# Beta factors loaded behind B's value weights, and phi's max(b,0) moved from VectorE to ScalarE

## The chip, the cores and the metric

The kernel runs on one core of one Trainium2 chip. The metric is the device time of one execution in microseconds (us); a kernel's time is the median of its runs. The core has five engines that run side by side, each through its own list of instructions in order: TensorE (PE; its weight loads are shown as PEld), VectorE (DVE), ScalarE (ACT), GpSimd (POOL) and SyncE (SP). DMA transfers are issued by SP, POOL or ACT and run on 16 DMA engines.

## The reference: what is computed

Two attention blocks over the same 2048 rows of 512 values, 32 heads of 16, mixed by a gate per row:

```python
x = A_x
g = _sigmoid((x * gate_w).sum(-1, keepdims=True))
a = _A_ref(x, A_wq, A_wk, A_wv, A_wo, A_beta)
b = _B_ref(x, B_wqkv, B_wo)
return g * a + (1 - g) * b
```

B is plain softmax attention over all 2048 rows. A works in four chunks of 512 rows. Inside a chunk it is causal attention (each row looks at itself and the rows ahead of it); across chunks a memory is carried, read with phi(q) and updated with phi(k):

```python
phi = lambda t: jnp.where(t > 0, t + 1.0, jnp.exp(t))
...
    num = jnp.einsum("bhld,bhde->bhle", pq, M)
    den = jnp.einsum("bhld,bhd->bhl", pq, z)[..., None] + 1e-6
    a_mem = num / den
    o = g * a_mem + (1.0 - g) * a_dot
    pk = phi(ks)
    M = M + jnp.einsum("bhld,bhle->bhde", pk, vs)
```

Here g is the sigmoid of one number per head, `A_beta`. In the kernel phi(t) is written as max(t,0) + min(exp(t),1), which is the same function.

## The kernel before: tiles, stages, queues

The order of the instructions on every engine is the order in which the code emits them; waits are put in where an instruction reads or overwrites what another engine made. There are three stages.

**Opening (to about 78 us).** x is loaded, A's values are projected, x is split in a high and a low half-precision part scaled by its largest absolute value. Then eight jobs `qk_job(3, "B", 0, w, c)` (L877) project B's queries and keys of the first group of heads. Beside them stand the preparations for what follows. Behind the third of these jobs VectorE takes the largest absolute values of A's first weights (`w_abs("A", 0)`, L884) and of the four pieces of B's value weights, k = 0 to 3 (`peak`, L366); behind the fourth, `top(("A", 0))` (L890) sends the result through a TensorE transpose (L383). TensorE's list goes no further before that one has run.

The four pieces of B's value weights are loaded by POOL (`load_wv`, L277), pieces 0 and 1 in the loop ahead (at `tt == 12`), pieces 2 and 3 behind the first qk_job (L881). Pieces 2 and 3 go into buffers that hold x's second chunk until VectorE has split its first half (L265). POOL's DMAs are issued in order, and an issue also waits until the eighth POOL DMA ahead of it has landed, since they share eight semaphores. On the same queue stand:

- `load_beta` (L225), twelve small DMAs that spread `A_beta` over the partitions into `gh` (4, L227) and `nq` (8, L230); `do_beta` (L235) makes the gate factors of them in the first block of the middle stage;
- `axk`, four DMAs `kb<-aux` (L181) that write constant rows into key buffer KB[0], which the score matmuls of the middle stage read;
- two more `qb<-aux` DMAs and, behind everything, the loads of A's second group of weights (L285).

**Middle stage (about 78 to 347 us).** Sixteen blocks, `blk` = 4 groups of heads x 4 chunks (L925). Each block projects A's queries (w = 0) and keys (w = 1) of its group and chunk with twelve matmuls each (L332), and between them runs the memory steps (`mem_out` reads the memory with phi(q): matmuls L436; `mem_tr` transposes phi(k): L461; `mem_upd`: L475, L480, L483), B's value projections (`v_job`, L302), B's other queries and keys, and from block 4 on first score maxima (`s_b`: matmuls L574, VectorE maximum L576). The function `qk_out` (L336) empties the PSUM bank b of a projection. Of the queries' and keys' 32 projections for A, 24 need phi. For such a one, before:

1. VectorE (L345): `ph = max(b*un, 0)`, from the bank;
2. ScalarE (L346): the high part `st[:, 0] = b*sc`, from the bank;
3. ScalarE (L348): `ex = exp(b*un)`, from the bank;
4. VectorE (L349): the low part `st[:, 1] = b*sc - st[:, 0]`, from the bank, after which the bank is free;
5. VectorE (L351): phi's sum `ph = min(ex, 1) + ph`, from SBUF, which `mem_out` or `mem_tr` reads.

Two engines never read one bank at a time: waits between the steps keep them in turn. `phe` (ex) has one buffer, phi one for w = 0 and one for w = 1, and `st` four, which come free when their two stores by SP (L355) have landed. From block 4 on the projections have four banks (tb, tb, mb, pvb), taken in the order in which they were last used.

**Main stage (from about 347 us).** 32 rounds, each with one unit of A's and one of B's attention: score matmuls L637, exponentials on ScalarE L643, value matmuls L659, and the next units' score maxima on VectorE (L576, L560, L562). Nothing of the change stands there.

Of the kernel before, what the change touches and what calls it, by code (L numbers as in the profile page):

```python
# [12 lines left out]
AF = mybir.ActivationFunctionType  # L13
OP = mybir.AluOpType
# [25 lines left out]
def gated_mix_kernel(ctx, tc, xt, wq, wk, wv, wo, beta, wqkv, wob, gate_w, out):  # L40
    nc = tc.nc
# [93 lines left out]
    def raw_buf():  # L135
        i = cnt.get("raw", 0)
        cnt["raw"] = i + 1
        return RAWV[i if i < 6 else 6 + (i - 6) % 8]
# [62 lines left out]
    def first_x(c, ks):  # L201
        first_split(xh[0][:, c % 2, ks], xl[c % 2][:, ks], XS[c][:, ks])
# [22 lines left out]
    def load_beta():  # L225
        for g in range(4):
            nc.gpsimd.dma_start(gh[:, g:g + 1], bass.AP(tensor=beta.tensor, offset=beta.offset + 8 * g,  # L227
                                                       ap=[[1, 8], [0, E], [1, 1]]))
        for qd in range(8):
            nc.gpsimd.dma_start(nq[:, qd:qd + 1], bass.AP(tensor=beta.tensor, offset=beta.offset + 4 * qd,  # L230
                                                         ap=[[1, 4], [0, 32], [1, 1]]))
# [35 lines left out]
    def wcols(kd, w):  # L267
        if kd == "A":
            return (wq, wk, wv)[w], 0
        return wqkv, w * DM  # L270
# [3 lines left out]
    def load_wv(kd, k, eng=None):  # L274
        src, c0 = wcols(kd, 2)
        WR[kd, "v", k] = raw_buf()
        (eng or nc.gpsimd).dma_start(WR[kd, "v", k], src[k * 128:(k + 1) * 128, c0:c0 + DM])  # L277
# [20 lines left out]
    def v_mm(b, kd, tt, n):  # L298
        xi, wi = TERMS[n // 4]
        c, tl = divmod(tt, 4)  # L300
        x = (XH, XL)[xi][c] if kd == "B" else (xh[0][:, c % 2], xl[c % 2])[xi]
        nc.tensor.matmul(b, x[:, n % 4, tl * 128:(tl + 1) * 128], (WVA if kd == "A" else WV)[wi][:, n % 4, :],  # L302
                         start=n == 0, stop=n == 11)

    def v_out(b, kd, tt):
        tl = tt % 4
        if tl % 2 == 0:
            rot("vs", VS)
        vs = VS[(cnt["vs"] - 1) % 2]
        b = b.rearrange("p (h e) -> p h e", h=H)  # L310
        if kd == "A":
            nc.scalar.activation(vs[:, tl % 2, :, :E], b, AF.Copy)
        else:
            nc.scalar.activation(vs[:, tl % 2, :, :E], b, AF.Copy, scale=vr[:, tt // 4:tt // 4 + 1])
        if tl % 2:
            nc.sync.dma_start(VD[kd][tt * 128 - 128:(tt + 1) * 128].rearrange("(a t) g h e -> t a (g h e)", a=2),
                              vs.rearrange("p a h e -> p a (h e)"))

    def v_job(kd, tt):
        b = misc()  # L320
        for n in range(12):
            v_mm(b, kd, tt, n)
        v_out(b, kd, tt)
# [12 lines left out]
    def qk_out(b, kd, g, w, c):  # L336

        sc = xr[:, c:c + 1]
        st = X.tile([128, 2, C], HF, name="st", bufs=4)
        phi = kd == "A" and (c > 0 if w == 0 else c < NC4 - 1)  # L340
        if phi:
            ph = PHI[g, w, c] = X.tile([128, C], FT, name=f"phi{w}")
            ex = X.tile([128, C], FT, name="phe")
            un = back[:, g, w, c:c + 1]
            nc.vector.tensor_scalar(ph, b, un, 0.0, op0=OP.mult, op1=OP.max)  # L345
        nc.scalar.activation(st[:, 0], b, AF.Copy, scale=sc)  # L346
        if phi:
            nc.scalar.activation(ex, b, AF.Exp, scale=un)  # L348
        nc.vector.scalar_tensor_tensor(st[:, 1], b, sc, st[:, 0], op0=OP.mult, op1=OP.subtract)  # L349
        if phi:  # L350
            nc.vector.scalar_tensor_tensor(ph, ex, 1.0, ph, op0=OP.min, op1=OP.add)  # L351
        img = QKD[kd, w, g][:, :, c * C:(c + 1) * C]
        for a in range(2):
            r = E * (a if w else 1 - a)
            nc.sync.dma_start(img[:, r:r + E], st[:, a])  # L355
        if w == 0 and c == 0:
            nc.sync.dma_start(QKD[kd, w, g][:, 2 * E:].rearrange("h r (n t) -> h r n t", t=64),
                              aux[:, 1, None, :].to_broadcast([E, 2 * NT, 64]))
# [14 lines left out]
    def x_abs(c):  # L373
        peak(stat(("B", 0), 6)[:, 2 + c:3 + c], XS[c])
# [421 lines left out]
    def todo(fn, *a):  # L796
        return lambda: fn(*a)
# [29 lines left out]
    axk = [todo(set_aux, KB[0][:, p], 0) for p in range(2)]  # L827
# [3 lines left out]
    for tt in range(NT):  # L831
        c, tl = divmod(tt, 4)
        if tt < 4:
            for n in range(4, 12):
                v_mm(vb[tt], "A", tt, n)
            v_out(vb[tt], "A", tt)
        else:
            v_job("A", tt)
        if c < 3 and tl < 2:
            first_x(c + 1, halves[tl])  # L840
        if tt in (1, 2, 5, 6):
            x_abs((1, 2, 5, 6).index(tt))
        if tt == 4:
            w_abs("B", 0)
        if tt == 9:
            top(("B", 0))
        if tt == 10:
            w_rng("B", 0)
            split_x(0, halves[0])
        if tt == 11:  # L850
            split_x(0, halves[1])
            x_all()
            w_esc("B", 0)
        if tt == 12:
            split_w(3, "B", 0)
        if tt in (13, 14):
            split_x(1, halves[tt - 13])
        if tt == 3:
            dot_x(0)
        if tt in (7, 12, 15):  # L860
            dot_x({7: 1, 12: 2, 15: 3}[tt])
        if tt == 11:
            load_w("A", 0)
        if tt == 12:
            load_wv("B", 0)
            load_wv("B", 1)
        if tt == 13:
            load_beta()
        if tt == 15:
            split_x(2, halves[0])  # L870
        if ax:
            ax.pop(0)()
    for f in axk:
        f()
    for n in range(8):
        c, w = divmod(n, 2)
        qk_job(3, "B", 0, w, c)  # L877
        if n < 3:
            split_x(2 + (n + 1) // 2, halves[(n + 1) % 2])
        if n == 0:  # L880
            load_wv("B", 2)  # L881
            load_wv("B", 3)
        if n == 2:
            w_abs("A", 0)  # L884
            for k in range(4):
                peak(s8[:, k:k + 1], WR["B", "v", k], AX.X)
            nc.vector.tensor_reduce(stat(("A", 0), 3)[:, 2:3], s8, axis=AX.X, op=OP.max)
            ST["A", 0] = ST["A", 0][0], 3
        if n == 3:
            top(("A", 0))  # L890
        if n == 4:
            w_rng("A", 0)
            split_w(0, "A", 0, (0,))
        if n == 5:
            w_esc("A", 0)
            v_rng()
            split_w(0, "A", 0, (1,))
        if n > 5:
            split_wv(2 * n - 12)
            split_wv(2 * n - 11)  # L900
        if n == 7:
            do_gate()
# [223 lines left out]
    ex = [extras(k) for k in range(32)]  # L1126
# [91 lines left out]
```

## Time and profile before

| | |
|---|---|
| median of 3 runs | 1846.14 us (1845.54 to 1846.72) |
| the profiled execution, its own time | 1847.55 us |
| its span in the trace | 1845.7 us |
| PE busy | 1790.1 us, 97% |
| DVE busy | 1607.8 us, 87% |
| ACT busy | 1445.5 us, 78% |
| POOL busy | 339.6 us, 18% |
| mean granted TensorE clock | 0.994 |

Times in the trace count from the span's start. A row of a timeline has start, length, engine, line, operation, what it writes and reads (out<-in), and in brackets how long its engine sat idle ahead of it and what ended that. A row of the waits has the waiting instruction, the one it waited for, the sum of us, how many times, and the longest. A row of the windows has, for a stretch, its length and the busy us of PE, PEld, DVE, ACT and POOL, then the clock granted to TensorE as a share of full speed. Rows that merge several instructions give their count (x8).

### The profile page before, as it was taken

What the parts mean: (1) busy time and instruction counts of PE and PEld (TensorE: products, weight loads), DVE (VectorE), ACT (ScalarE), POOL (GpSimd) and SP (SyncE); (2) the same over time, 40 slices, a digit from 0 to 9 for tenths busy, and PEclk for the clock granted to TensorE, in tenths of its full rate; (3) what the DMA queues carried; (4) which work ended last, traced back from release to release, by engine and by line L of the source; (5) the groups of instructions that cost most, each with busy time, mean ns of one, the idle gap of its engine ahead of it and who ended that gap; (6) DMA issues with size and microseconds to landing.
All of it is one profiled execution on the core that took longest, in us unless ns stands there. A gap on an engine that the chain in (4) does not pass through costs nothing.

```text
span 1845.7 us, 44303 instructions
## 1 busy us (share of the span) xinstructions
PE 1790.1 (97%) x17781; PEld 644.8 (35%) x17781; DVE 1607.8 (87%) x1811; ACT 1445.5 (78%) x2717; POOL 339.6 (18%) x691
## 2 busy tenths in 40 slices
PE   8799989899999999999999999999999999999998
PEld 6454444322222222333333333333333333333325
DVE  7645786699999999999999999999999999999942
ACT  4433333388989999989898989898989898989894
POOL 4400000101212010212121212121212121212122
PEclk9899999999999999999999999999999999999999
DMA  5645533332323222223232323232323232323111
GB/s 194 130 127 151 159 87 107 91 98 74 93 73 92 63 82 62 80 67 86 67 86 67 85 67 86 68 86 67 86 68 86 68 86 68 87 69 87 46 39 61
DMA packets 162482, 158.92 MB, mean 86 GB/s; under 512 B 40140, under 2 KB 126620, under 8 KB 162276
## 3 DMA queue, kind: packets, MB, share of 16 engines
q1 hardware_dynamic: 158692, 149.29, 29.1%
q0 software_dynamic: 3296, 6.27, 1.8%
q8 instruction: 140, 2.29, 0.5%
q14 instruction: 66, 0.54, 0.1%
q10 hardware_dynamic: 288, 0.52, 0.1%
HBM read 103.38 MB, written 50.86 MB: 84 GB/s over the span
## 4 chain that ended last, share of the span: by engine, by line
PE 72%; DVE 19%; ACT 5%; issue 2%; DMA 2%; SPq 0%; ACTq 0%; DVEq 0%; POOLq 0%
PE pvb L659 27%; DVE mxb L576 14%; PE tb L637 11%; PE sbk L574 9%; PE mb L637 6%; ACT raw L643 3%; PE tb L744 2%; PE tb L332 2%; PE sbk L552 2%; PE mb L332 2%; PE tb L302 1%; PE pvb L332 1%; PE mb L744 1%; PE sbk L302 1%; PE sbk L332 1%
## 5 line engine op out<-in xcount | busy, mean ns | idle before, releaser
L576 DVE TENSOR_REDUCE mxb<-sbk 128x2 f32<-128x1024 f32 x1024 | 1172.3, 1211 | 21.1 <-PE sbk L574 10.4
L643 ACT ACTIVATE raw<-tb 128x512 f32<-128x512 f32 x1555 | 884.1, 600 | 62.6 <-PE tb L637 25.6
L659 PE MATMUL pvb<-raw,vb 128*17 128x256 f32 (+1 forms) x8072 | 644.6, 388 | 0.0
L574 PE MATMUL sbk<-kb,qb 64*128 64x512 f16 x2048 | 552.9, 377 | 9.2 <-DVE mxb L576 8.2
L643 ACT ACTIVATE raw<-mb 128x512 f32<-128x512 f32 x782 | 469.1, 600 | 32.9 <-PE mb L637 16.9
L637 PE MATMUL tb<-qb,kb 64*128 64x512 f16 x1342 | 467.7, 380 | 2.4 <-ACT raw L643 1.3
L637 PEld LDWEIGHTS <-kb 64*128 64x128 f16 x2048 | 143.2, 93 | 413.3 <-issue 409.3
L659 PEld LDWEIGHTS pvb<-raw,vb 128*17 128x17 f32 x8072 | 137.9, 95 | 402.9 <-issue 393.6
L637 PE MATMUL mb<-qb,kb 64*128 64x512 f16 x679 | 258.4, 381 | 0.0
L646 POOL TENSOR_SCALAR_AFFINE_SELECT raw<-raw 128x256 f32<-128x256 f32 (+1 forms) x320 | 115.4, 361 | 324.3 <-ACT raw L643 315.9
L574 PEld LDWEIGHTS <-qb 64*128 64x128 f16 x2048 | 137.1, 93 | 45.6 <-issue 35.2
L560 DVE TENSOR_REDUCE mx<-sbk 128x2 f32<-128x1024 f32 (+1 forms) x128 | 133.9, 1087 | 6.7 <-PE sbk L556 5.6
L659 PE MATMUL pvb<-raw,va 128*17 128x256 f32 (+2 forms) x1280 | 103.2, 383 | 3.7 <-ACT pvs L668 0.9
L703 POOL TENSOR_TENSOR o<-o,d 128x512 f32<-128x512 f32 x31 | 39.4, 1272 | 218.7 <-DMA d<-rd 156.9
L562 DVE TENSOR_REDUCE mx<-sbk 128x4 f32<-128x512 f32 x64 | 60.6, 947 | 12.5 <-PE sbk L556 12.5
L552 PE MATMUL sbk<-ka,qa 64*128 64x512 f16 (+3 forms) x512 | 70.8, 296 | 0.0
L346 ACT ACTIVATE st<-tb,xr 128x512 f16<-128x512 f32 x28 | 19.2, 687 | 59.2 <-DVE phi L345 30.3
L637 PE MATMUL tb<-qa,ka 64*128 64x512 f16 (+3 forms) x339 | 62.0, 302 | 0.0
L691 POOL TENSOR_TENSOR rec<-rec,grow 128x16 f32<-128x16 f32 x24 | 5.3, 222 | 275.7 <-DVE rec L683 275.7
L332 PEld LDWEIGHTS <-ws 128*128 128x128 f16 x384 | 37.6, 99 | 44.5 <-issue 4.8
L556 PE MATMUL sbk<-cmask,crows 64*128 64x64 bf16 x1024 | 52.8, 189 | 0.0
L556 PEld LDWEIGHTS <-crows 64*128 64x128 bf16 x1024 | 46.5, 94 | 13.8
(358 smaller groups left out, 1621.8 us busy)
## 6 DMA issues: line engine op xcount, KB each, us to landing
vb<-vdB SPq DMA_DIRECT2D x16, 1088.0 KB
pd<-pvs SPq DMA_DIRECT2D x64, 256.0 KB
kb<-dB SPq DMA_DIRECT2D x60, 256.0 KB
dB<-st SPq DMA_DIRECT2D x64, 128.0 KB
dA<-st SPq DMA_DIRECT2D x64, 128.0 KB
o<-pd SPq DMA_DIRECT2D x64, 128.0 KB
d<-rd SPq DMA_DIRECT2D x63, 128.0 KB
kb<-dB SPq DMA_DIRECT2D x60, 128.0 KB
```

The source lines that it names most:

```text
L332: nc.tensor.matmul(b, WS[ws][w][wi][:, k, :], (XH, XL)[xi][c][:, k, :], start=n == 0, stop=n == 11)
L552: nc.tensor.matmul(b[:, j, c0:c0 + n], q_of(u)[r, p, i * 128:(i + 1) * 128], k_of(u, p)[r, :n], start=True, stop=False)
L556: nc.tensor.matmul(b[:, j, c0 + n - 128 + w.start:c0 + n - 128 + w.stop], crows[r, n2 - 1], cmask[r, n2 - 1, w], start=False, stop=n2 == 2)
L560: nc.vector.tensor_reduce(m[:, :, p, i], b[:, :, :n], axis=AX.X, op=OP.max)
L562: nc.vector.tensor_reduce(m[:, :, :, i], b.rearrange("q j (p k) -> q j p k", p=2)[:, :, :, :n], axis=AX.X, op=OP.max)
L574: nc.tensor.matmul(b[:, j], q_of(u)[r, p, i * 128:(i + 1) * 128], k_of(u, p)[r, kc * C:(kc + 1) * C], start=True, stop=True)
L576: nc.vector.tensor_reduce(MXB[u][:, :, p, i, kc], b, axis=AX.X, op=OP.max)
L637: nc.tensor.matmul(bs[j][:, c0:c0 + w], k_of(u, h // 2)[r, 128 * it:128 * it + 128], q_of(u)[r, h // 2, q0:], start=True, stop=True)
L643: nc.scalar.activation(pt, bs[j], AF.Exp, scale=AT["esc", kd, qd // 2])
L646: nc.gpsimd.affine_select(out=m, in_=m, pattern=[[1, 128]] if n < 2 else [[0, 2], [1, 128]], compare_op=OP.is_ge, fill=0.0, base=0, channe ...
L659: nc.tensor.matmul(PVB[32 * h:32 * h + E + 1, q0 + lo:q0 + hi], vt[:, it, 4 * q + h, :], pt[:, lo:hi], start=it == 0 and lo == 0, stop=it ...
L744: nc.tensor.matmul(b[j], (AT["oh"], AT["ol"])[oi][r, g, a], (AT["wh"], AT["wl"])[wi][r, g, a], start=n == 0, stop=n == 11)
```

## The change

Two things are moved, and nothing else: what is computed stays the same.

**The loads.** `load_beta` and `axk` are taken from where they stood and put behind `load_wv("B", 2)` and `load_wv("B", 3)`.

**qk_out.** Step 1 goes to ScalarE as a Relu with the same scale, in front of the exponential; the high part comes behind both, and phi's sum ahead of the low part.

```diff
             un = back[:, g, w, c:c + 1]
-            nc.vector.tensor_scalar(ph, b, un, 0.0, op0=OP.mult, op1=OP.max)
+            nc.scalar.activation(ph, b, AF.Relu, scale=un)
+            nc.scalar.activation(ex, b, AF.Exp, scale=un)
+            nc.vector.scalar_tensor_tensor(ph, ex, 1.0, ph, op0=OP.min, op1=OP.add)
         nc.scalar.activation(st[:, 0], b, AF.Copy, scale=sc)
-        if phi:
-            nc.scalar.activation(ex, b, AF.Exp, scale=un)
         nc.vector.scalar_tensor_tensor(st[:, 1], b, sc, st[:, 0], op0=OP.mult, op1=OP.subtract)
-        if phi:
-            nc.vector.scalar_tensor_tensor(ph, ex, 1.0, ph, op0=OP.min, op1=OP.add)
...
-        if tt == 13:
-            load_beta()
...
-    for f in axk:
-        f()
...
         if n == 0:
             load_wv("B", 2)
             load_wv("B", 3)
+            for f in axk:
+                f()
+            load_beta()
```

How POOL's list changes in the opening (a count behind x merges equal issues; `raw<-in_B_wqkv` 128x512 are the value weights' pieces, `in_A_wq` and `in_A_wk` A's weights):

```order
 L277 DMA raw_86<-in_B_wqkv_dram 128x512 x2
-L181 DMA qb_70<-aux 16x8x64 x2
+L181 DMA qb_70<-aux 16x8x64 x4
+L277 DMA raw_86<-in_B_wqkv_dram 128x512 x2
+L181 DMA kb_89<-aux 16x32x64 x4
 L227 DMA gh<-in_A_beta_dram 128x1x1 x4
 L230 DMA nq<-in_A_beta_dram 128x1x1 x8
-L181 DMA qb_70<-aux 16x8x64 x2
-L181 DMA kb_89<-aux 16x32x64 x4
-L277 DMA raw_86<-in_B_wqkv_dram 128x512 x2
 L285 DMA raw_86<-in_A_wq_dram 128x4x128
```

Pieces 2 and 3 stood behind 18 other DMAs after pieces 0 and 1; now four `qb<-aux` stand between, and the twelve beta loads and the four `kb<-aux` come behind.

VectorE's list in block 2, where the bank tb1 holds the queries' and the bank mb the keys' projection, before:

```order
L345 TENSOR_SCALAR phi0_988<-tb1_135,back_128 128x512
L349 SCALAR_TENSOR_TENSOR st_987<-tb1_135,xr_126,st_987 128x512
L351 SCALAR_TENSOR_TENSOR phi0_988<-phe_989,phi0_988 128x512
L345 TENSOR_SCALAR phi1_1018<-mb_137,back_128 128x512
L349 SCALAR_TENSOR_TENSOR st_1017<-mb_137,xr_126,st_1017 128x512
L351 SCALAR_TENSOR_TENSOR phi1_1018<-phe_1019,phi1_1018 128x512
```

and after, in the changed kernel's line numbers (L347 is phi's sum there):

```order
L481 TENSOR_TENSOR mtmp_970<-tb0_134,bmask_115 128x136
L347 SCALAR_TENSOR_TENSOR phi0_988<-phe_989,phi0_988 128x512
L349 SCALAR_TENSOR_TENSOR st_987<-tb1_135,xr_126,st_987 128x512
L347 SCALAR_TENSOR_TENSOR phi1_1018<-phe_1019,phi1_1018 128x512
L349 SCALAR_TENSOR_TENSOR st_1017<-mb_137,xr_126,st_1017 128x512
```

VectorE has one operation less for each of the two, and phi's sum stands ahead of the low part. ScalarE's list at the same place, after (L345 is the Relu, L346 the exponential, L348 the high part, L436 and L437 the copies of `mem_out`):

```order
L345 ACTIVATE phi0_988<-tb1_135,back_128 128x512
L346 ACTIVATE phe_989<-tb1_135,back_128 128x512
L348 ACTIVATE st_987<-tb1_135,xr_126 128x512
L345 ACTIVATE phi1_1018<-mb_137,back_128 128x512
L346 ACTIVATE phe_1019<-mb_137,back_128 128x512
L348 ACTIVATE st_1017<-mb_137,xr_126 128x512
L436 ACTIVATE recm_1028<-sbk0_138 128x16
```

Before it had the high part and the exponential for each, in that order; now three operations follow each other on ScalarE ahead of the copies of `mem_out`.

## The prediction

> **What bounds the kernel now.** I read the windows by stage first, then what TensorE waits for in the opening and middle stages, then the timelines at the longest waits. The windows:
>
> ```profile
> 66.70:78.30 11.60, 0.03 (x1) 0.03 (x2) 4.45 (x9) 0.69 (x1) 3.88 (x6) 0.72 0.75 182
> 78.30:347.00 268.70, 252.35 (x1339) 128.14 (x1340) 171.64 (x320) 96.19 (x189) 15.87 (x26) 0.98 0.43 122
> 347.00:374.00 27.00, 22.98 (x143) 7.38 (x142) 16.52 (x17) 12.64 (x22) 0.00 (x0) 0.94 0.20 57
> 374.00:1800.00 1426.00, 1414.74 (x15822) 442.57 (x15818) 1352.76 (x1364) 1284.04 (x2421) 275.67 (x569) 1.00 0.28 76
> ```
>
> From 66.7 to 78.3 TensorE stands still. From there to 347 it is busy 252.35 of 268.70 us, VectorE only 64%, ScalarE 36%: TensorE's list sets the pace and its idle time is 16.35 us. In the main stage TensorE (99%) and VectorE (95%) are full, and the change touches nothing there; each round starts from what the round ahead left, so an earlier start should move the end by as much. So the question is how much of 11.6 + 16.35 us goes. TensorE's waits from 60 to 347 us (those of at least 1 us in a row):
>
> ```profile
> PE pvb L383 <- DVE stat L887: 11.6, 1, 11.6
> PE tb L436 <- DVE phi L351: 2.9, 4, 1.0
> PE tb L302 <- DVE st L349: 2.5, 2, 1.3
> PE mb L436 <- DVE phi L351: 2.4, 2, 1.4
> PE mb L332 <- DVE st L349: 1.7, 1, 1.7
> PE tb L436 <- DVE mst L480: 1.5, 2, 1.0
> PE sbk L574 <- DVE mxb L576: 1.3, 2, 0.7
> PE tb L332 <- DVE st L349: 1.1, 2, 0.6
> PE sbk L436 <- DVE phi L351: 1.1, 1, 1.1
> ```
>
> So there are four kinds: one long wait for the weights' maximum; 2.9 + 2.4 + 1.1 = 6.4 us in which `mem_out` waits for phi; 1.5 us for the memory state behind it; 2.5 + 1.7 + 1.1 = 5.3 us for a bank that the low part (L349) has not yet freed.
>
> **The load order: minus 7.1 us.** The long wait, on TensorE, VectorE and POOL:
>
> ```profile
> 65.64 1.03 PE L332 MATMUL sbk<-xq,wt 128*128 128x512 f16 x4
> 78.27 0.59 PE L383 MATMUL pvb<-ident,stat 128*3 128x128 f32 x2 [11.60 <-DVE stat L887]
> 78.79 3.55 PE L332 MATMUL sbk<-xp,wt 128*128 128x512 f16 x8
> ```
>
> ```profile
> 53.66 1.28 DVE L265 SCALAR_TENSOR_TENSOR xq<-raw,xu,xp 128x1024 f16<-128x1024 f32 x1
> ...
> 67.08 2.46 DVE L366 TENSOR_REDUCE stat<-raw 128x1 f32<-128x512 f32 x4
> 76.63 1.39 DVE L366 TENSOR_REDUCE stat<-raw 128x1 f32<-128x512 f32 x2 [7.09 <-DMA raw<-in_B_wqkv_dram]
> 78.06 0.16 DVE L887 TENSOR_REDUCE stat<-stat 128x1 f32<-128x4 f32 x1
> ```
>
> ```profile
> 50.29 1.09 POOL L181 DMA_DIRECT2D qb<-aux  x2
> 51.45 2.61 POOL L227 DMA_DIRECT2D gh<-in_A_beta_dram  x4
> 54.30 5.42 POOL L230 DMA_DIRECT2D nq<-in_A_beta_dram  x8 [0.24 <-DMA raw<-in_B_wqkv_dram]
> 62.65 0.55 POOL L181 DMA_DIRECT2D qb<-aux  x1 [2.92 <-DMA nq<-in_A_beta_dram]
> ...
> 68.35 0.57 POOL L277 DMA_DIRECT2D raw<-in_B_wqkv_dram  x1
> ```
>
> VectorE takes four maxima in a row, then idles 7.09 us for pieces 2 and 3, because piece 2 was issued only at 68.35, behind the beta loads and POOL's waits for their landing. In the new order four `qb<-aux` (1.09 us for two) run from 50.29 to about 52.5. Piece 2's buffer is free when the split that starts at 53.66 ends, at 54.94, so it is issued at about 55.0 and piece 3 at 55.6. Before, piece 2 was in use 76.63 - 68.35 = 8.3 us after its issue; so both are there by about 64, and VectorE asks for them at 67.08 + 2.46 = 69.5. The margin is over 5 us, and without it the gain shrinks us for us. What is late next is VectorE itself: six maxima and L887 one after the other end at 78.2 - 7.1 = 71.1 us, so TensorE still stands still for some 4.5 us.
>
> What is moved back: the four `kb<-aux` (first read when the score matmuls begin, in block 4) follow at 56 to 59, then the twelve beta issues (2.61 + 5.42 us here). POOL's waits for landings come with them; from the last beta issue at 59.7 these lasted until piece 2 was issued at 68.35, some 9 us. So the factors land near 59 + 8 + 2 + 9 = 78. They are asked for by `do_beta`:
>
> ```profile
> 99.62 0.20 ACT L235 ACTIVATE gh<-gh 128x4 f32<-128x4 f32 x1
> ```
>
> that is at 92.5 after the shift: 14 us of cover, so they cost nothing; were it gone, ScalarE would stand at L235 with every bank copy queued behind it. A's second weights come behind beta as before, at about the same time, and are read in block 1, later still. SP's queue is not changed. The bounds of the term are 0 (pieces late again) and 7.1, plus or minus the clock, below.
>
> **phi: minus 7.9 us on its own waits.** One pair of projections in block 2 shows the chain:
>
> ```profile
> 122.25 1.89 PE L332 MATMUL tb<-xp,ws 128*128 128x512 f16 x8
> 123.98 1.03 PE L332 MATMUL tb<-xq,ws 128*128 128x512 f16 x4
> ...
> 128.69 1.17 PE L436 MATMUL sbk<-mst,phi 128*128 128x136 f32 x8 [1.10 <-DVE phi L351]
> ```
>
> ```profile
> 125.12 0.75 DVE L345 TENSOR_SCALAR phi<-tb,back 128x512 f32<-128x512 f32 x1 [2.37 <-PE tb L332]
> 125.90 0.69 ACT L346 ACTIVATE st<-tb,xr 128x512 f16<-128x512 f32 x1 [4.05 <-DVE phi L345]
> 126.49 0.68 ACT L348 ACTIVATE phe<-tb,back 128x512 f32<-128x512 f32 x1
> ...
> 127.20 0.75 DVE L349 SCALAR_TENSOR_TENSOR st<-tb,xr,st 128x512 f16<-128x512 f32 x1 [1.33 <-ACT phe L348]
> 127.87 0.68 DVE L351 SCALAR_TENSOR_TENSOR phi<-phe,phi 128x512 f32<-128x512 f32 x1
> ```
>
> The bank is full at 125.01. VectorE, ScalarE twice, VectorE twice: phi is ready at 128.55, 3.5 us later. New: the Relu has no row here; its nearest rows are the exponential (0.68) and the high part (0.69), the same size from the same bank, and I take 0.68 (bounds 0.59, the step from one to the next, and 0.75, VectorE's own time for it). ScalarE's operations follow at 0.59 (126.49 - 125.90). So Relu at 125.1, exponential 125.7 to 126.4, phi's sum on VectorE 126.4 to 127.1: ready 2.1 us after the bank is full, 1.4 us earlier. `mem_out` waits at seven places, 0.9 us on the mean and 1.4 at most, so it finds phi ready (6.4 us). The memory state (L480) stands behind these steps on VectorE, which loses 0.75 us and an idle wait per projection: 1.5 us go. Bounds: 0 to 7.9; below nothing is a rival.
>
> ScalarE gains 24 operations of 0.68, 16 us in 268.7, and goes from 36% to 42%; VectorE loses 24 of 0.75, 18 us, and goes from 64% to 57%. Their cover is that idle time; nothing of it is on TensorE's path except through the banks.
>
> **The bank: minus 2.8 us.** The bank now passes from ScalarE (three operations, 0.1 + 0.59 + 0.59 + 0.69) to VectorE's low part (0.75): free at 125.01 + 2.75, before at 127.95, 2.94 after. That is only 0.2 us by itself; more is won where VectorE's queue held the first step up, since ScalarE no longer waits for it. Two of the five places:
>
> ```profile
> 173.40 1.89 PE L302 MATMUL tb<-wv,xp 128*128 128x512 f16 x8 [1.29 <-DVE st L349]
> ...
> 191.58 3.46 PE L302 MATMUL tb<-wv,xp 128*128 128x512 f16 x8 [1.18 <-DVE st L349]
> ```
>
> At the first, the second projection's steps queue behind the first's on VectorE, and without that the release comes some 1.8 us earlier: 1.29 go. At the second, TensorE itself arrives 0.5 us earlier (phi's wait ahead of it is gone) and the release comes about 1 us earlier: some 0.5 go. I take about half of 5.3 for all, 2.8; bounds 0 and 5.3. The waits for L576 stay.
>
> **Sum.** 7.1 + 7.9 + 2.8 = 17.8 us, against the profiled execution's 1847.55 (its span and 1.85 us around it): 1829.75. That execution is 1.41 us above the median, so 1846.14 - 17.8 = 1828.3.
>
> **The clock,** by this trace:
>
> ```profile
> 187.97:191.38 3.41, 1.95 (x14) 1.38 (x11) 2.08 (x4) 1.90 (x6) 0.00 (x0) 1.00 0.28 77
> 191.38:194.79 3.41, 3.21 (x8) 1.16 (x8) 3.38 (x6) 0.06 (x1) 0.00 (x0) 0.50 0.28 77
> ```
>
> Behind the long wait, eight matmuls took 3.55 us instead of the 1.89 at 122.25, and at 191.58 they took 3.46: 1.7 and 1.6 us lost at half clock. The second time TensorE had been busy for 57% of the 3.4 us ahead. So idle stretches far shorter than 4.5 us are enough, and I keep the first loss in the sum, as in before. The Trainium skill, "TensorE: Matmul & The Clock Gate", section "Part 1: The HAM clock gate", has the clock fall after a whole idle window of some 3.4 us, of windows that run freely. By that rule a stop of 4.5 us often holds no whole window; the row at 187.97 speaks against it.
>
> **Rivals.**
>
> *The clock stays up at both places.* The rest at 71 us is too short to cool, and the waits that cooled at 191 are gone. For it: two waits of 0.5 and 1.2 us shrink there. Against it: the rows above, for the first. 17.8 + 1.7 + 1.6 = 21.1: 1825.0. This is what the skill's rule would give.
>
> *Only the loads count.* phi comes earlier, but the waits move to the bank, to L576 or to ScalarE's copies. For it: half of the bank's waits remain by my own working. Against: TensorE's next bank is usually the oldest of four. Minus 7.1: 1839.0.
>
> *The pieces land late again,* behind x's and B's stores, and only phi counts: minus 10.7, 1835.4. Against: over 5 us of margin.
>
> *Nothing reaches the end,* because the main stage starts from something else than TensorE (a transfer, the key loads): 1846.1. Against: 23 of 27 us are TensorE's in the stretch between.
>
> *ScalarE sets the pace: slower.* In the middle stage each bank now waits for three ScalarE operations in a row, and ScalarE's list also holds the value copies and weight splits. If each of the 24 Relus came fully on top of the bank's release, 24 x 0.68 = 16.3 us come on and no wait of phi goes: 16.3 - 7.1 = 9.2 slower, 1855.3. It decides from the point where ScalarE starts on a full bank more than 1.4 us late on the mean; at 42% busy with pieces of 0.7 us it does not.
>
> **Numbers.** Forecast 0.70; clock up 0.08; loads alone 0.10; pieces late 0.05; nothing reaches the end 0.04; ScalarE 0.03. The first four are faster: 0.93; same 0.04; slower 0.03 (0.2%, 3.7 us, is about what a measurement of this kernel can tell from no change). The range starts where all 16.35 us of idle time and the 7.1 go (1822.7) and reaches to the loads alone (1839.0).
>
> **What would show it.** Right: piece 2 issued near 55 us; no VectorE idle ahead of the last two maxima; L383 at 71 to 71.5 us; L436 without waits for phi; the main stage's first L637 some 18 us earlier, and the rounds behind it as long as before. Wrong: L383 later than 72; TensorE's idle time in the middle stage still over 10 us; ScalarE named as the releaser of TensorE's waits; or an earlier start that is lost again in the main stage.

## The result, and the profile after

The changed kernel takes 1825.04 us (median of 4 runs, 1824.12 to 1825.88), the kernel before in the same session 1845.89 us: a ratio of 0.9886, 95% interval 0.9869 to 0.9903, or 20.9 us less. The profiled execution took 1825.88 us, its span is 1824.2 us.

The windows by stage of the changed kernel, in the columns of the prediction's first table (length, then busy us of PE, PEld, DVE, ACT and POOL, granted clock):

```profile
66.80:71.20 4.40, 0.10 (x2) 0.04 (x2) 4.37 (x9) 0.69 (x1) 2.59 (x4) 0.74 0.82 34
71.20:324.80 253.60, 247.49 (x1341) 128.23 (x1341) 155.18 (x296) 109.98 (x214) 16.66 (x27) 0.99 0.48 133
...
354.00:1778.00 1424.00, 1413.62 (x15815) 442.33 (x15814) 1351.20 (x1363) 1283.25 (x2418) 275.49 (x569) 1.00 0.28 76
```

TensorE's stop at 67 us has shrunk from 11.6 to 4.3 us. Its idle time in the middle stage has shrunk from 16.35 to 253.60 - 247.49 = 6.11 us. VectorE's busy time there went from 64% to 61%, ScalarE's from 36% to 43%. The main stage is as full as it was.

The load place in the changed kernel, from the timeline (POOL's issues, then VectorE's maxima and TensorE's transpose):

```profile
55.43 1.11 POOL L277 DMA_DIRECT2D raw<-in_B_wqkv_dram  x2 [2.84 <-DVE xq L265]
...
67.28 3.64 DVE L364 TENSOR_REDUCE stat<-raw 128x1 f32<-128x512 f32 x6
...
71.16 0.59 PE L381 MATMUL pvb<-ident,stat 128*3 128x128 f32 x2 [4.30 <-DVE stat L884]
71.68 3.59 PE L332 MATMUL sbk<-xp,wt 128*128 128x512 f16 x8
```

Pieces 2 and 3 are issued at 55.43 us (68.35 before), the six maxima run in one piece, and the transpose starts at 71.16 us, 7.11 us earlier. Eight matmuls behind it still take 3.59 us, at half clock, as before. The beta factors cost nothing: ScalarE takes them up (L235) without waiting.

```profile
91.37 0.20 ACT L235 ACTIVATE gh<-gh 128x4 f32<-128x4 f32 x1
```

TensorE's waits in the changed kernel from 60 us to the start of the main stage (sum, times, longest; left out are 1.3 us for score maxima and 0.2 for a bank):

```profile
PE pvb L381 <- DVE stat L884: 4.3, 1, 4.3
PE tb L302 <- DVE st L349: 1.8, 2, 1.1
PE tb L332 <- DVE st L349: 1.4, 2, 1.0
...
PE mb L332 <- DVE st L349: 1.0, 1, 1.0
```

Every wait of `mem_out` (L434 now, L436 before) is gone: 6.4 us for phi and the listed 1.5 for the memory state. The bank's waits (L349) have only gone from 5.3 to 1.8 + 1.4 + 1.0 = 4.2 us.

The chain from bank to phi in block 2, at the place that the prediction showed, in the timeline of the changed kernel:

```profile
114.99 1.03 PE L332 MATMUL tb<-xq,ws 128*128 128x512 f16 x4
115.86 1.89 PE L332 MATMUL mb<-xp,ws 128*128 128x512 f16 x8
116.06 0.69 ACT L345 ACTIVATE phi<-tb,back 128x512 f32<-128x512 f32 x1 [3.19 <-PE tb L332]
116.64 0.68 ACT L346 ACTIVATE phe<-tb,back 128x512 f32<-128x512 f32 x1
...
117.36 0.69 DVE L347 SCALAR_TENSOR_TENSOR phi<-phe,phi 128x512 f32<-128x512 f32 x1 [3.59 <-ACT phe L346]
...
117.97 0.75 DVE L349 SCALAR_TENSOR_TENSOR st<-tb,xr,st 128x512 f16<-128x512 f32 x1
118.45 1.09 PE L434 MATMUL sbk<-mst,phi 128*128 128x136 f32 x8
```

The bank is full at 116.02 us and phi is ready at 118.05, 2.03 us later (3.5 before), and 0.40 us before the first matmul that reads it starts at 118.45, without a wait. How much of that is room can be read from before: there TensorE waited for phi and started 0.14 us after it was ready (128.55 to 128.69), so the room here is about 0.26 us. The Relu takes 0.69 us.

The main stage's first score matmuls, before and after:

```profile
347.36 0.39 PE L637 MATMUL tb<-qb,kb 64*128 64x512 f16 x1
```

```profile
324.86 0.39 PE L635 MATMUL tb<-qb,kb 64*128 64x512 f16 x1
```

They start 22.5 us earlier. From there to the end of the span it was 1845.7 - 347.36 = 1498.3 us, and is now 1824.2 - 324.86 = 1499.3. So the whole account is:

| from the two traces | us |
|---|---|
| transpose of the weights' maximum earlier (78.27 to 71.16) | -7.1 |
| idle time of TensorE in the middle stage (16.35 to 6.11) | -10.2 |
| half clock in the middle stage | -3.1 |
| fewer new starts of TensorE behind a stop (remainder) | -2.1 |
| main stage, itself 1.0 longer | +1.0 |
| span | -21.5 |

The half clock comes from the stretches with granted clock 0.5: before, 78.8 to 82.16, 95.81 to 99.22 and 191.38 to 194.79 us with TensorE at work, which at half speed loses half of 10.2 us, 5.1; after, 71.7 to 75.76 alone, 2.0. The remainder fits what one stop costs beyond its listed wait. Before, in block 2:

```profile
124.84 1.89 PE L332 MATMUL mb<-xp,ws 128*128 128x512 f16 x8
```

From there to `mem_out`'s first matmul at 128.69 (its row stands in the prediction) are 3.85 us with a wait of 1.10; after, without it, 115.86 to 118.45 are 2.59. The wait cost 1.26, 0.16 more than its row says. Twelve stops of the list before are gone (ten of L436, two of L383); if each cost as much, an estimate from this one place, that is 1.9 of the 2.1 us.

### The profile page after: what moved, and what is told of

It reads as the page before. It is cut to its first block, busy times and chain, and to the rows that moved or that the text cites. A ratio compares the mean times of both kernels' runs of the same rounds, so it can differ in the third digit from the quotient of the medians.

```text
span 1824.2 us, 44323 instructions
## 1 busy us (share of the span) xinstructions
PE 1786.8 (98%) x17781; PEld 645.1 (35%) x17781; DVE 1590.9 (87%) x1787; ACT 1459.3 (80%) x2741; POOL 339.5 (19%) x691
## 4 chain that ended last, share of the span: by engine, by line
PE 78%; DVE 14%; ACT 4%; issue 2%; DMA 1%; POOL 0%; SPq 0%; ACTq 0%; DVEq 0%; POOLq 0%
PE pvb L657 28%; DVE mxb L574 12%; PE tb L635 12%; PE sbk L572 9%; PE mb L635 6%; PE tb L332 3%; ACT raw L641 3%; PE tb L742 2%; PE mb L332 2%; PE sbk L550 2%; PE tb L302 2%; PE sbk L302 2%; PE pvb L332 2%; PE mb L742 1%; PE sbk L332 1%
## 5 line engine op out<-in xcount | busy, mean ns | idle before, releaser
L574 DVE TENSOR_REDUCE mxb<-sbk 128x2 f32<-128x1024 f32 x1024 | 1172.5, 1212 | 21.7 <-PE sbk L572 11.1
L572 PE MATMUL sbk<-kb,qb 64*128 64x512 f16 x2048 | 552.7, 378 | 8.4 <-DVE mxb L574 7.3
L572 PEld LDWEIGHTS <-qb 64*128 64x128 f16 x2048 | 137.4, 93 | 44.3 <-issue 33.7
L347 DVE SCALAR_TENSOR_TENSOR phi<-phe,phi 128x512 f32<-128x512 f32 x24 | 16.6, 692 | 51.6 <-ACT phe L346 51.6
```

The lines of the kernel that those rows point to most:

```text
L572: nc.tensor.matmul(b[:, j], q_of(u)[r, p, i * 128:(i + 1) * 128], k_of(u, p)[r, kc * C:(kc + 1) * C], start=True, stop=True)
L574: nc.vector.tensor_reduce(MXB[u][:, :, p, i, kc], b, axis=AX.X, op=OP.max)
```

## Experiments

Twelve kernels in four sessions, each timed against the kernel before in its own session, whose median went from 1846.57 to 1847.09 us. "After" stands for the changed kernel; its line numbers shift by one or a few in some of the kernels.

| kernel | median, us | ratio to before (95% interval) |
|---|---|---|
| loads alone | 1837.15 | 0.9952 (0.9935 to 0.9968) |
| new qk_out alone | 1835.15 | 0.9938 (0.9921 to 0.9954) |
| after, phi's sum behind the low part | 1833.45 | 0.9926 (0.9909 to 0.9942) |
| after, max back on VectorE, in front | 1827.44 | 0.9896 (0.9879 to 0.9912) |
| after, Relu twice | 1834.60 | 0.9923 (0.9902 to 0.9944) |
| after, key buffer's rows ahead of the pieces | 1824.88 | 0.9875 (0.9858 to 0.9892) |
| after, beta loads ahead of the pieces | 1830.32 | 0.9904 (0.9887 to 0.9921) |
| after, keys' phi by way of a copy | 1826.92 | 0.9895 (0.9876 to 0.9913) |
| after, transpose one job later | 1820.47 | 0.9854 (0.9834 to 0.9875) |
| ... and products moved, maxima earlier | 1820.54 | 0.9863 (0.9847 to 0.9880) |
| ... and the keys' copy as well | 1822.35 | 0.9872 (0.9853 to 0.9891) |
| ... without the keys' copy, sums taken apart | 1817.66 | 0.9844 (0.9831 to 0.9858) |

### One half of the change each

The loads alone, that is the changed kernel with qk_out as before:

```diff
-            nc.scalar.activation(ph, b, AF.Relu, scale=un)
-            nc.scalar.activation(ex, b, AF.Exp, scale=un)
-            nc.vector.scalar_tensor_tensor(ph, ex, 1.0, ph, op0=OP.min, op1=OP.add)
+            nc.vector.tensor_scalar(ph, b, un, 0.0, op0=OP.mult, op1=OP.max)
...
```

> The loads moved as in the change, qk_out as before. My theory (the waits that end with phi and with the bank, and the load wait, are separate terms): the long wait of TensorE goes from 11.6 to 4.3 us, the waits for phi stay at some 6 us; 7.1 us less than before, 1838.8 us. Clock theory: some 3.4 us either way of that, by how many half-clock stretches the profile shows between 66 and 360 us (before had four, the change two). Rival, only the loads count: as the changed kernel, 1825.

Measured: 1837.15 us, 9.75 less than before's 1846.90. The profile has the 4.3 us and all the waits for phi:

```profile
PE pvb L383 <- DVE stat L886: 4.3, 1, 4.3
PE tb L436 <- DVE phi L351: 2.9, 4, 1.0
```

The new qk_out alone, that is the changed kernel with the loads where they stood before:

```diff
+        if tt == 13:
+            load_beta()
...
+    for f in axk:
+        f()
...
-            for f in axk:
-                f()
-            load_beta()
```

> The new qk_out with the loads as before. My theory: the long wait stays at 11.6 us, the waits for phi and for the memory state (7.9 us) go, those for the bank shrink by 1.2; 9 to 14 us less than before, 1832 to 1837 us, the rest by the clock stretch at 191 us that goes with them. Rival, only the loads count: 1846.

Measured: 1835.15 us, 11.75 less. The long wait is back at 12.6 us and no wait of `mem_out` is left:

```profile
PE pvb L381 <- DVE stat L885: 12.6, 1, 12.6
```

The two halves add up to 21.5 us; the change gave 20.9. So they are separate terms, and the rival "only the loads count" falls. The loads alone gave 2.7 us more than the 7.1 that the transpose moved; their trace has a single half-clock stretch from 66 to 300 us, 72.05 to 75.46, where before lost the clock three times with TensorE at work, once (at 191.38) behind a wait that this kernel still has. That the same wait cost the clock in one execution and not in the other shows how much hangs on where the windows of the clock happen to lie (last section).

### Is it phi's time or VectorE's work?

Phi's sum back behind the low part, with VectorE's work as light as in the change:

```diff
-            nc.vector.scalar_tensor_tensor(ph, ex, 1.0, ph, op0=OP.min, op1=OP.add)
         nc.scalar.activation(st[:, 0], b, AF.Copy, scale=sc)
         nc.vector.scalar_tensor_tensor(st[:, 1], b, sc, st[:, 0], op0=OP.mult, op1=OP.subtract)
+        if phi:
+            nc.vector.scalar_tensor_tensor(ph, ex, 1.0, ph, op0=OP.min, op1=OP.add)
```

> The changed kernel with phi's sum put back behind the low part; VectorE has the same work as in the change. My theory (what counts is when phi is ready): phi is ready 3.4 us after the bank is full instead of 2.1, nearly as late as before (3.5), so most of the 6.4 us of waits for phi come back: 1830 to 1834 us. Rival (what counts is the 18 us of work taken from VectorE): as the changed kernel, 1825 to 1827.

Measured: 1833.45 us. The waits of `mem_out` (L435 here) are back, in the list of TensorE's waits of this kernel:

```profile
PE mb L435 <- DVE phi L350: 1.6, 2, 0.8
...
PE tb L435 <- DVE phi L350: 1.3, 3, 0.8
PE sbk L435 <- ACT phi L345: 0.8, 1, 0.8
PE tb L435 <- ACT st L347: 0.8, 1, 0.8
PE tb L435 <- DVE mst L479: 0.7, 1, 0.7
PE tb L382 <- DVE stat L365: 0.7, 1, 0.7
PE pvb L382 <- DVE stat L365: 0.5, 1, 0.5
```

The five rows of L435 are 5.2 us together. (The rows that name ScalarE are the same wait: in block 2 phi's sum ran from 119.19 to 119.87 us and L435 started at 120.02.) The last two rows, waits for the maxima of the next weights, stood in before's list too and are not in after's.

The other way round, the maximum on VectorE and both orders as in the change:

```diff
-            nc.scalar.activation(ph, b, AF.Relu, scale=un)
+            nc.vector.tensor_scalar(ph, b, un, 0.0, op0=OP.mult, op1=OP.max)
```

> The changed kernel with max(b,0) back on VectorE, in front; the exponential ahead of the high part and phi's sum ahead of the low part as in the change. VectorE has all the work that it had before. My theory (what counts is when phi is ready): phi is ready some 2.3 us after the bank is full, the waits for phi stay away, those for the bank grow by up to 2: 1825 to 1829 us. Rival (what counts is the work taken from VectorE): the waits come back, 1834 to 1838 us.

Measured: 1827.44 us. VectorE has all its old work and the waits for phi stay away; phi is ready 2.3 us after the bank is full. The waits for the next weights' maxima stay away too, so they go with the order and not with VectorE's lighter list. The two kernels answer the question: it is the order behind the bank, exponential first and phi's sum first, that brings most of the time. For the move to ScalarE itself 2.4 us are left by the medians, and the intervals of this kernel and of the change overlap. Its trace has 2.5 + 1.9 + 1.2 = 5.6 us of waits for the bank, where before had 5.3 and the change has 4.2, so what the move takes away is waits for the bank; and it has a half-clock stretch at 88.07 us, worth 1.7 us, that the change's trace does not have.

### Does ScalarE set the pace?

```diff
             nc.scalar.activation(ph, b, AF.Relu, scale=un)
+            nc.scalar.activation(ph, b, AF.Relu, scale=un)
```

> The changed kernel with every Relu of phi done twice, which leaves the result as it is: 0.59 us more of ScalarE for each of the 24 projections, in front of the exponential. My theory (ScalarE has slack; only the chain from bank to phi grows, from 2.1 to 2.7 us): a part of the waits comes back, 1826 to 1830 us. Rival (ScalarE sets the pace of the middle stage): 24 x 0.59 = 14 us come on, 1839 us.

Measured: 1834.6 us, 9.6 more than after: between the two, and my size was wrong. TensorE's waits, to be held against after's list above:

```profile
PE tb L302 <- DVE st L350: 3.3, 2, 1.8
PE mb L332 <- DVE st L350: 1.7, 1, 1.7
PE tb L332 <- DVE st L350: 1.6, 2, 1.1
...
PE mb L435 <- DVE phi L348: 0.6, 2, 0.3
...
```

The row for phi stands for three with 1.5 us together. All waits of the list together are 5.2 us more than after's 10.0, 2.4 of them for the bank. And a half-clock stretch is back at 181.02, and another stands in the main stage at 426.78 us, 1.7 us each. ScalarE's queue is not what TensorE waits for; the chain behind a full bank is. Phi had about 0.26 us of room in block 2 (above), and the second Relu makes it ready 2.74 us after the bank is full instead of 2.03; 0.7 us more is past that room, and the waits for phi are 0.3 us at a time.

### What held the pieces of the weights?

The key buffer's constant rows ahead of pieces 2 and 3 instead of behind them:

```diff
         if n == 0:
+            for f in axk:
+                f()
             load_wv("B", 2)
             load_wv("B", 3)
-            for f in axk:
-                f()
             load_beta()
```

> The changed kernel with the four constant rows of the key buffer issued ahead of B's value weights' pieces 2 and 3, and only the beta factors behind them. My theory (the beta loads held the pieces, and there are over 5 us of margin): no change, 1825 us, the long wait at 4.3 us. Rival (any DMA ahead of the pieces costs its landing): 2 to 6 us more.

Measured: 1824.88 us, no change; the pieces are issued at 55.44 us all the same, since in the change POOL waits 2.84 us for their buffer there (its row at 55.43 us) and the four issues fit into that gap. With the beta loads there:

```diff
         if n == 0:
+            load_beta()
             load_wv("B", 2)
             load_wv("B", 3)
             for f in axk:
                 f()
-            load_beta()
```

> The changed kernel with the twelve beta loads put back ahead of pieces 2 and 3, and only the four constant rows behind them. My theory (the beta loads held the pieces): 8 us of issues and the waits for their landing stand ahead of piece 2, which is issued at 64 to 67 us; the long wait is 8 to 11 us, 1829 to 1832 us. Rival (the constant rows held them): as the changed kernel, 1825 us.

Measured: 1830.32 us. From its timeline:

```profile
64.25 0.57 POOL L277 DMA_DIRECT2D raw<-in_B_wqkv_dram  x1 [2.40 <-DVE st L349]
...
71.77 0.69 DVE L364 TENSOR_REDUCE stat<-raw 128x1 f32<-128x512 f32 x1 [1.71 <-DMA raw<-in_B_wqkv_dram]
...
74.09 0.59 PE L381 MATMUL pvb<-ident,stat 128*3 128x128 f32 x2 [6.89 <-DVE stat L884]
```

Piece 2 is issued 8.8 us later than after's and VectorE waits for it again; the stop is 6.9 us, a little less than I had expected, and the time in the range. So the beta loads by themselves hold the pieces, and the constant rows by themselves do not. But this is not all of the long wait: with all loads as before (the new qk_out alone) the stop is 12.6 us and the time 1835.15. There, six `aux` issues stand between the beta loads and the pieces, and some of them wait for a landing of a beta load (the prediction's row at 62.65 us shows one such wait, of 2.92), so that piece 2 is issued at 68.99 us, 4.7 later than here. It takes the beta loads and the rows queued behind them to make the whole wait. (In before, 2 + 4 + 8 + 2 + 4 = 20 issues stood between pieces 1 and 2, not 18.)

### The waits for the bank

For the keys alone (w = 1), the exponential and phi's sum come behind the low part and read phi's tile, not the bank; all else is as in the change:

```diff
-            nc.scalar.activation(ph, b, AF.Relu, scale=un)
+            nc.scalar.activation(ph, b, AF.Copy if w else AF.Relu, scale=un)
+        if phi and w == 0:
...
+        if phi and w == 1:
+            nc.scalar.activation(ex, ph, AF.Exp)
+            nc.vector.tensor_scalar(ex, ex, 1.0, None, op0=OP.min)
+            nc.vector.scalar_tensor_tensor(ph, ph, 0.0, ex, op0=OP.max, op1=OP.add)
```

> The changed kernel with another way to phi for the keys' projections alone (w = 1): ScalarE copies the scaled bank into phi's tile, then makes the high part; the low part on VectorE then frees the bank, and only then come the exponential (from phi's tile), its minimum with 1 on VectorE and phi's sum. So the bank is read three times instead of four, and phi of the keys is ready some 1.2 us later. My theory of the waits for the bank that are left (TensorE comes back to a bank some 1.8 us after it was filled, and the chain of four reads holds it 2.7 us): the chain is 0.6 us shorter, the four waits of 0.5 to 1.1 us shrink by 0.5 each, the windows stay free of half clock: 2 us less, 1823 us. Rival (VectorE's queue holds the low part): no change or worse, since VectorE gets 12 operations more: 1825 to 1827 us.

Measured: 1826.92 us. The time is the rival's, the mechanism mine. The changed kernel at the largest of these waits:

```profile
157.81 1.03 PE L332 MATMUL tb<-xq,ws 128*128 128x512 f16 x4
...
158.88 0.69 ACT L345 ACTIVATE phi<-tb,back 128x512 f32<-128x512 f32 x1 [1.67 <-PE tb L332]
...
160.79 0.75 DVE L349 SCALAR_TENSOR_TENSOR st<-tb,xr,st 128x512 f16<-128x512 f32 x1
...
161.59 1.67 PE L302 MATMUL tb<-wv,xp 128*128 128x512 f16 x7 [1.07 <-DVE st L349]
```

The bank is full at 158.84 us and free at 161.54: three operations of ScalarE and one of VectorE, each started as soon as the one ahead is done. TensorE is back at this bank after 1.7 us, because only short matmuls stand between (L572, L249, L434), and waits out the chain. The kernel with the copy:

```profile
161.46 1.89 PE L302 MATMUL tb<-wv,xp 128*128 128x512 f16 x8 [0.47 <-DVE st L350]
168.73 0.38 PE L386 MATMUL pvb<-ident,stat 128*2 128x128 f32 x2 [0.96 <-DVE stat L369]
```

The waits for the bank went from 1.07 to 0.47 here, from 0.77 to 0.17 at the next place, and from 0.97 to 0.37 at a third: 0.6 each, one read less. The other two, 0.48 and 0.96 us, stayed as they were. There the projection has no phi, and the low part waits for VectorE: in the changed kernel at the second of them (319.15 us) the bank is full at 316.72, two score maxima (L574) hold VectorE from 316.09 to 318.44, and the low part starts at 318.35. In exchange TensorE now waits for what VectorE makes of the next weights (0.96 us here, 1.2 and 0.7 at two other places). Twelve more minima stand on VectorE, and the keys' sum stands behind the low part again; which of the two does it was not tried. Won 1.8, lost 2.9.

### What is late next at the load place

```diff
-        if n == 3:
+        if n == 4:
             top(("A", 0))
-        if n == 4:
+        if n == 5:
             w_rng("A", 0)
             split_w(0, "A", 0, (0,))
-        if n == 5:
+        if n == 6:
             w_esc("A", 0)
```

> The changed kernel with the transpose of the weights' maximum, and what follows from it, emitted one projection job later, so that four more matmul pairs of B's queries and keys stand in front of it on TensorE. My theory: 2.6 of the 4.3 us that TensorE stands still at 67 to 71 us are filled: 2.6 us less, 1822.4 us. Clock theory: with a stop of only 1.7 us the half clock behind it goes too, 1.7 to 3.4 us more: 1819 to 1821 us. Rival (VectorE's list is late anyway): no change, 1825 us.

Measured: 1820.47 us. From its timeline:

```profile
70.47 0.38 PE L381 MATMUL sbk<-ident,stat 128*3 128x128 f32 x2 [1.71 <-DVE stat L884]
70.78 1.90 PE L332 MATMUL tb<-xp,wt 128*128 128x512 f16 x8
```

The stop is 1.71 us and the eight matmuls behind it take 1.90 us instead of 3.59: full clock. The main stage starts at 319.39 us, 5.5 earlier than after's: 2.6 of the stop, some 2 of the clock, and 0.7 because this execution's maxima ran 0.7 us earlier.

Next, the rest of the stop:

```diff
-        if tt in (7, 12, 15):
-            dot_x({7: 1, 12: 2, 15: 3}[tt])
+        if tt in (7, 12):
+            dot_x({7: 1, 12: 2}[tt])
...
-        if n == 2:
+        if n == 0:
             w_abs("A", 0)
-            for k in range(4):
+        if n == 1:
+            for k in range(2):
                 peak(s8[:, k:k + 1], WR["B", "v", k], AX.X)
+        if n == 2:
+            for k in range(2, 4):
+                peak(s8[:, k:k + 1], WR["B", "v", k], AX.X)
...
         if n == 4:
             top(("A", 0))
+            dot_x(3)
```

> The kernel with the transpose one job later, and besides the last quarter of the gate's products (four VectorE operations, 3.0 us, at 57 us) put behind the transpose, and the maxima of A's weights and of pieces 0 and 1 taken one or two jobs earlier, in the place that this frees. My theory: VectorE has only two maxima left behind the last split, the weights' maximum is ready at 69 instead of 70.3 us, and the 1.7 us in which TensorE still stands go: 1818.5 to 1819 us. Rival (the products are then late for the gate's sums at 79 us): the wait moves there, 1820 to 1822 us.

Measured: 1820.54 us: nothing more. The time is in the rival's range, but not by its mechanism. The transpose ran at 68.65 us with a wait of 0.24, 1.8 us earlier, and the products came in time. What took it back, in the windows of this kernel and in its timeline:

```profile
76.93:80.34 3.41, 3.41 (x32) 3.37 (x30) 3.12 (x13) 3.35 (x6) 0.00 (x0) 1.00 0.51 174
80.34:83.75 3.41, 3.41 (x11) 1.61 (x12) 3.41 (x6) 1.65 (x4) 0.00 (x0) 0.50 0.41 132
```

```profile
77.16 1.84 PE L221 MATMUL mb<-one,phi 128*128 128x1 f32 x16
78.86 1.03 PE L221 MATMUL mb<-one,om 128*128 128x1 f32 x8
79.75 1.32 PE L221 MATMUL mb<-one,pk 128*128 128x1 f32 x8
80.94 3.27 PE L332 MATMUL sbk<-xp,ws 128*128 128x512 f16 x8
```

A window in which TensorE is busy all the time, but nearly only with the one-column matmuls of the gate's sums, is followed by one at half clock: the last one-column piece takes 1.32 us (0.29 more than the one ahead of it) and the eight matmuls 3.27, 1.38 more than at full clock, together 1.7 us. The main stage starts at 319.23 us, 0.16 earlier than with the transpose alone. The keys' copy on top of this:

> Both of the two kernels ahead in one: the transpose one job later with the products behind it, and the keys' phi by way of a copy. My theory: the terms add up, 1.7 and 2 us below the kernel with the transpose one job later alone: 1816.5 to 1817.5 us. Rival (the keys' path does nothing): 1819 us.

Measured: 1822.35 us, 1.8 above the kernel without the copy; by itself the copy had cost 1.9 (1826.92 against 1825.04). So neither of the two expected gains came.

The last kernel takes the one-column matmuls apart, behind the transpose and the products as moved:

```diff
-    def sum_x():
-        b = misc()[:, :NT]
-        for tt in range(NT):
+    def sum_x(c):
+        if c == 0:
+            SX.append(misc()[:, :NT])
+        b = SX[0]
+        for tt in range(4 * c, 4 * c + 4):
...
+        if n > 3:
+            sum_x(n - 4)
         if n == 7:
             do_gate()
```

> The kernel with the transpose one job later and the products moved, and besides the one-column matmuls of the gate's sums (32 in a row on TensorE, 3.7 us) taken apart into four pieces of eight, one behind each of the last four projection jobs, the piece of chunk c behind job 4 + c. Clock theory (a window of 3.41 us that holds little else than one-column matmuls counts as idle, and the next window has half clock): no half clock between 66 and 300 us, the eight matmuls behind the last piece take 1.9 instead of 3.3 us: 1.4 us less, main stage from 317.8 us, 1819.1 us. Rival (what cools TensorE there is something else, a transfer or VectorE): half clock stays near 80 us, 1820.5 us.

Measured: 1817.66 us, the median of 5 runs. From its timeline:

```profile
81.83 1.89 PE L335 MATMUL sbk<-xp,ws 128*128 128x512 f16 x8
```

The same eight matmuls take 1.89 us, and the trace has no half clock between 60 and 328 us. From the transpose to the main stage it is 318.74 - 69.82 = 248.9 us, in the kernel ahead 319.23 - 68.65 = 250.6: the 1.7 us are back. So the clock theory held at this place. By the medians this kernel is 2.9 us below the one ahead, with intervals that overlap; of the 2.0 us between the two profiled executions 1.5 lie behind the start of the main stage, where half clock lasts one window instead of two. With a ratio of 0.9844 (0.9831 to 0.9858) this version beats before, and its interval lies below the change's.

## Why the prediction was right, and where it was off

The forecast was 1828.3 us, the measurement 1825.04: the direction, the mechanism and the main terms held, and 17.8 us were forecast where the two profiled executions differ by 21.7. Part of what came on top is luck (the clock, below).

- **The load term, 7.1:** held as worked out. Issue at 55.43 (about 55.0), no gap before the last two maxima, the transpose at 71.16 (71.1), TensorE's stop 4.3 (4.5). The beta loads, with the constant rows queued behind them, held the pieces, and both were in time in their new place.
- **phi, 7.9:** held. Phi is ready 2.03 us after the bank (2.1), and all of these waits are gone; the two kernels that take the order and VectorE's load apart show that the order does it. I had not said that most of it comes from the order and little from the move to ScalarE.
- **The bank, 2.8:** this is the term that was mis-sized; 1.1 came. The step that failed is "at the first, the second projection's steps queue behind the first's on VectorE": before, L345 started on that bank at 170.52 us, 0.08 us after it was full. There was no queue to win from, and the wait went from 1.29 to 1.07 us. What sets it is that TensorE comes back to the bank 1.7 us after filling it, while the chain of four reads holds it 2.7 us; the kernel with three reads took 0.6 us off at this and two more of the five places. At the other two VectorE's list does hold the low part up, behind work that the change did not touch (1.66 before and 0.96 now at one, 0.48 both times at the other); and at one place the wait grew, from 0.64 to 0.97.
- **Not in the sum:** 1.2 us of TensorE's waits for the next weights' maxima (L383 behind L366, 0.7 and 0.5 us in before's waits) went as well. They are back with phi's sum behind the low part, and stay away with the maximum on VectorE, so it is the order that takes them away; how it does so was not followed. With them the idle time adds up: 7.9 + 1.1 + 1.2 = 10.2 us. And the one stop that was measured cost 0.16 us beyond its listed wait.
- **The clock:** I kept the loss behind the long wait, and it stayed (3.59 us for eight matmuls). I said nothing of the stretch at 95.81 and did not count on that at 191.38 going; both went, 1.7 us each. The first is luck: the same one-column matmuls still stand in a row, and in after's execution a border between two windows happens to part them (last section). The second is missing in the trace of the loads alone too, which keep the wait ahead of it, so it need not come from the change either. The main stage took 1.0 us more; its half clock lasts from 331.76 to 338.58 us, two windows, where before had one, 355.22 to 358.63. The rival "the clock stays up at both places" gave 1825.0, the time that came, but not by its mechanism: at 71 us the clock did not stay up.
- **Rivals:** the loads alone, the pieces late again and nothing reaching the end are excluded by the profile and the halves. ScalarE as the pace is not what the profile shows, but the point from which its operations count was nearer than I had it: I gave the chain 1.4 us of room, the trace has some 0.26 in block 2, and 0.7 us more on the chain, with the clock lost at two more places, cost 9.6 us.

## What to carry to other kernels

When a consumer waits for the last of several steps behind a full bank, look at their order before their engine: what the consumer needs goes first. The slack left is the time from the moment the result is ready to the consumer's start, less what the consumer takes to start when it does wait. Small loads that wait for each other's landing, put ahead of a large one on one queue, cost the consumer of the large one; move them to where nobody waits. A stop that is shortened may still cost half clock behind it, so fill it with independent work, and look at the granted clock before and after each change.

## What the runs showed of the hardware

**When the clock falls.** The half-clock stretches up to 400 us are always whole multiples of 3.41 us and lie on one grid of windows per execution. A window need not be idle for the next to be slow. The kernel with two Relus has both cases:

```profile
160.54:163.95 3.41, 1.62 (x12) 0.96 (x11) 2.28 (x3) 2.47 (x8) 0.00 (x0) 1.00 0.52 164
163.95:167.36 3.41, 3.41 (x19) 1.83 (x18) 3.25 (x8) 1.18 (x2) 0.00 (x0) 1.00 0.25 72
177.61:181.02 3.41, 1.92 (x14) 1.57 (x13) 2.17 (x4) 2.84 (x8) 0.00 (x0) 1.00 0.28 77
181.02:184.43 3.41, 3.41 (x10) 1.18 (x8) 3.23 (x7) 0.00 (x0) 0.00 (x0) 0.50 0.28 77
```

1.62 busy us of 3.41 kept the clock, 1.92 lost it, so busy time alone does not decide. In the fourteen profiles of this case, from 60 to 385 us, every window up to 40% busy was followed by half clock; between 42 and 57% it went either way. The Trainium skill, "TensorE: Matmul & The Clock Gate", section "Part 1: The HAM clock gate", puts the fall behind at least one idle window of some 3.4 us, and has the window run freely, without a new start for each kernel. The traces agree on the length, 3.41 us, and on the free running: half clock first begins at 71.92 us in before, at 71.00 with the maximum on VectorE and at 69.36 with phi's sum behind the low part, which are no multiples of 3.41 apart. That the window must be idle they do not bear out, by the row with 1.92 busy us.

**A window full of one-column matmuls loses the clock.** Behind 3.2 us of them in one window (busy 3.41 of 3.41 by the trace) the clock was 0.50; in four pieces of 1 us with large matmuls between it stayed at full. Before had the same loss at 95.81 us:

```profile
92.40:95.81 3.41, 3.41 (x28) 2.81 (x29) 2.29 (x5) 1.16 (x3) 0.00 (x0) 1.00 0.52 138
95.81:99.22 3.41, 3.41 (x10) 1.21 (x9) 0.00 (x0) 0.19 (x1) 0.00 (x0) 0.50 0.45 132
```

From full clock, no window over 60% busy lost it except six, each filled to 0.65 or more by these matmuls. In the seven other profiles that have the 32 of them in a row, no window holds more than 0.61 of its length of them, and the clock stayed: in the changed kernel a border at 86.00 us parts them into 1.54 and 2.09 us. So with the 32 in a row it is left to the windows' position whether 1.7 us are lost; taken apart, at most 0.31 of a window was theirs. That fits one-column matmuls not counting as work, but what exactly counts was not tried further.
